# Cosine attention and a feed-forward layer on one core: each batch's values, second products and first products regrouped into one visit

## The chip, the cores and the metric

The kernel runs on one core of a Trainium2 chip. A core has TensorE (matrix products, called PE in the profile, with its weight loads as PEld), VectorE (DVE), ScalarE (ACT), GpSimd (POOL) and SyncE (SP, which here only starts transfers). The metric is the device time of one execution in microseconds (us), as the median of several runs; lower is better. Before the change it is 428.98 us, the median of 3 runs (428.75, 428.98 and 428.99).

## The reference

Per batch (8) and head (12), with 448 tokens of 64 numbers each, rows of q and k are divided by their norms, scores are their products divided by tau = 0.1, and a softmax over the keys weighs the rows of v. The heads side by side give 3584 rows of 768 numbers, which go through two matrix products with a leaky relu between them.

```python
q_n = q / (np.linalg.norm(q, axis=-1, keepdims=True) + 1e-06)
k_n = k / (np.linalg.norm(k, axis=-1, keepdims=True) + 1e-06)
scores = np.matmul(q_n, k_n.transpose(0, 1, 3, 2)) / tau
scores = scores - np.max(scores, axis=-1, keepdims=True)
attn = np.exp(scores)
attn = attn / (np.sum(attn, axis=-1, keepdims=True) + 1e-09)
attn_out = np.matmul(attn, v)
...
h = x @ w_in                       # 768 to 2048
g = np.maximum(0.01 * h, h)
return (g @ w_out).astype(np.float32)   # 2048 to 768
```

## The kernel before, in words

**Units of work.** Two heads make a pair, or slot; there are 6 slots a batch, 48 in all, numbered through. Two slots make a quad: 3 a batch, 24 in all. A batch's 448 keys are three tiles of 128 and a rest of 64. `s0` stands below for a batch's first slot, `b * NPAIR`.

**Norms of a slot.** `load_qk` (L122) loads q and k. POOL squares them (`squares`, L158, recorded at L167), after a small copy (`hold`, L484) that waits until the slot before is normed. DVE sums the squares (`sums`, L171, recorded at L178). ACT takes the roots with a Ln and an Exp (`roots`, L182: L185, L186). DVE divides (`normalise`, L192: L197, L198, L202). From slot 12 on, a transfer on SP's queue transposes the result into a tile qkT (`transposes`, L228: L234), of which there are five. `norm(s)` (L645) is all of this for slot s, the loads three slots on and the squares of the next slot. In it, sums come directly before the roots.

**Key tiles.** `key_tiles` (L247) multiplies keys with queries into two PSUM banks per tile (recorded at L259) and then has ACT take the exponential of each (L271) into pe, or pr for the rest. A tile of 128 keys uses the array as 64 rows by 128 columns, two heads side by side. The tile called (p, 3) holds the 64 rest keys of slots p-1 and p, as four products of 64 rows by 64 columns.

**Values.** `attend(j)` (L570) does quad j: `totals` sums the exponentials over keys (4 x 4 strips of 128 rows by 32 columns, recorded at L282), ACT inverts them with a Ln and an Exp (L293, L294), `products` multiplies with the values in two groups of 4 x 4 strips (L282 too), and `scale` (L308: L313) has DVE multiply both into xT.

**The two products of the feed-forward layer.** Chunk c holds 384 (c even) or 512 (c odd) of the tokens; chunk 2m+1 also takes the rest rows of batch 2m. `first(c, m)` (L327) is one of 16 blocks of hidden units: 6 products of 128 rows by 128 columns (L336), whose leaky relu ACT takes (L343). `second(c, ts, half)` (L362) does half of the outputs of a block of 128 tokens: 16 products of 128 by 128 (L366), copied out by DVE (L377). `both_halves` (L392) does the same block in another form: each product is split into two of 64 rows, side by side (L415), 32 in the first part and 32 in the second; in the second part the row halves change banks, so its first product waits for the last of the first part. DVE then copies both halves out (L425), and SP stores them (L388).

**PSUM.** `banks` (L79) deals out the eight banks, always the ones that were dealt or given back longest ago; two next to each other for a key tile, for `attend` and for `both_halves`. A token block of `both_halves` keeps its two until they are copied out.

**The order.** Every engine runs its instructions in the order in which the code issues them, which is written out by hand. Batches 0 to 2 have stages of their own (L514 to L694). From batch 3 on, a loop (L704) makes three visits per batch. The first belongs to the last quad of the batch before. Each visit is: `attend` of a quad; two key tiles; the first part of a token block; three key tiles; its second part; two key tiles, the last of them with rest keys; then a `norm`, half of the visit's first products of the chunk of the batch before (5 or 6 blocks), another `norm`, and the other half. Where a chunk has four token blocks, the fourth goes between the first products as two `second`. Behind the last batch come the last quad, the remaining token blocks as `second`, and the last chunk.

SP's queue holds, in that order, transposes, loads and stores. A transfer waits there for its data and for its buffer, and those behind it wait with it. POOL's queue holds squares and the loads of values (`load_v`, L141; `load_v_rem`, L148).

Of the kernel before, what the change touches and what calls it, by code (L numbers as in the profile page):

```python
# [8 lines left out]
F32 = mybir.dt.float32  # L9
# [7 lines left out]
def kernel(  # L17
# [10 lines left out]
    nc = tc.nc  # L28
    B, H, S, D = q.shape
    N_tok, D_model = out.shape  # L30
# [6 lines left out]
    NPAIR = H // 2  # L37
    NSLOT = B * NPAIR
    NQ = NPAIR // 2
    KT = D_model // 128  # L40
    MT = D_ff // 128
    HALF = D_model // 2
# [6 lines left out]
    MT_APART = 1  # L49
# [7 lines left out]
    smp = ctx.enter_context(tc.tile_pool(name="small", bufs=3))  # L57
    qnp = ctx.enter_context(tc.tile_pool(name="qn", bufs=3))
    qtp = ctx.enter_context(tc.tile_pool(name="qt", bufs=5))
    pep = ctx.enter_context(tc.tile_pool(name="pe", bufs=3))  # L60
    prp = ctx.enter_context(tc.tile_pool(name="pr", bufs=2))
    rbp = ctx.enter_context(tc.tile_pool(name="rb", bufs=2))
    xtp = ctx.enter_context(tc.tile_pool(name="xt", bufs=2))
    htp = ctx.enter_context(tc.tile_pool(name="ht", bufs=2))
    osp = ctx.enter_context(tc.tile_pool(name="os", bufs=3))
# [13 lines left out]
    def banks(count, keep=None, which=None):  # L79
        lo, hi = (0, 8) if not deals["apart"] else (0, 4) if count == 2 else (4, 8)  # L80
        x = which if which is not None else min(
            (i for i in range(lo, hi, count) if not set(range(i, i + count)) & set(sum(kept.values(), []))),
            key=lambda i: max(age[i : i + count]),
        )
        deals["n"] += 1
        age[x : x + count] = [deals["n"]] * count
        if keep:
            kept[keep] = list(range(x, x + count))
        return ps[:, x] if count == 1 else ps[:, x : x + count]

    def given_back(keep):
        deals["n"] += 1
        for i in kept.pop(keep):
            age[i] = deals["n"]
# [44 lines left out]
    vb, vrb = {}, []  # L139

    def load_v(j):  # L141
        if j >= B * NQ:
            return
        b, jj = divmod(j, NQ)
        vb[j] = vbp.tile([128, 4, 3, D], BF16, name="v_b")
        gp.dma_start(out=vb[j], in_=main(v, b, 4 * jj, 4))

    def load_v_rem(b):  # L148
        if b >= B:
            return  # L150
        r = v[b, :, MAIN:S].rearrange("(j g) p d -> g p j d", g=4)
        for g in range(4):
            lo = 64 * (g // 2)
            gp.dma_start(out=vrb[b % 2][lo : lo + 64, :, g], in_=r[g])
# [16 lines left out]
    def sums(s, parts=(0, 1)):  # L171
        if s >= NSLOT:
            return
        if s not in ss:
            ss[s] = smp.tile([128, 14], F32, name="ss")
        for i in parts:
            o = ss[s][:, 0:8] if i == 0 else ss[s][:, 8:14]
            nc.vector.tensor_reduce(  # L178
                o.rearrange("p (h t) -> p h t", h=2), sqs[s][i], axis=AX.X, op=ALU.add
            )  # L180
# [61 lines left out]
    pe, pr = {}, {}  # L242
# [79 lines left out]
    def chunk_cols(c):  # L322
        return (0, MAIN) if c % 2 == 0 else (MAIN, 512)
# [25 lines left out]
    osb = {}  # L349
# [12 lines left out]
    def second(c, ts, half):  # L362
        c0, n = chunk_cols(c)
        po2 = banks(1)
        for m in range(MT):
            nc.tensor.matmul(  # L366
                out=po2[:, :HALF],
                lhsT=hT[c][:, m, ts * 128 : (ts + 1) * 128],
                rhs=w_out_sb[:, m, half * HALF : (half + 1) * HALF],
                start=(m == 0), stop=(m == MT - 1),  # L370
            )
        if half == 0:
            osb[c, ts] = osp.tile([128, D_model], F32, name="osb")
        o = osb[c, ts]
        last = c == B - 1 and ts == n // 128 - 1
        cut = HALF // 2 if last and half == 1 else HALF
        nc.vector.tensor_copy(out=o[:, half * HALF : half * HALF + cut], in_=po2[:, :cut])  # L377
        if cut < HALF:
            nc.scalar.copy(out=o[:, half * HALF + cut : (half + 1) * HALF], in_=po2[:, cut:HALF])
        if half == 1 or last:  # L380
            store(o, c, c0 + ts * 128, half * HALF if last else 0, (half + 1) * HALF, cut < HALF)

    def store(o, c, x, lo, hi, apart=False):
        end, row = x + 128, 0
        while x < end:
            dst, cnt = rows_of(c, x, end)
            eng = nc.scalar if apart and row else nc.sync
            eng.dma_start(out=dst[:, lo:hi], in_=o[row : row + cnt, lo:hi])  # L388
            x += cnt
            row += cnt  # L390

    def both_halves(c, ts):  # L392

        state = {}

        def part(n):
            if n == 0:
                state["po"] = banks(2, ("rows", c, ts))  # L400
            po2 = state["po"]
            last = {}
            for m in range(MT):
                for h in range(2):
                    rows, half = slice(64 * h, 64 * h + 64), h ^ n
                    if n == 1 and m == 0:
                        tc.add_manual_dep(
                            nc.tensor.nop().ins,
                            state["last"][half].ins.name,
                            mybir.DependencyInfo(  # L410
                                mybir.DependencyClass.Sync, mybir.DependencyReason.DATA
                            ),
                            reason="the other rows' products in this bank",
                        )
                    last[half] = nc.tensor.matmul(  # L415
                        out=po2[:, half, :HALF],
                        lhsT=hT[c][rows, m, ts * 128 : (ts + 1) * 128],
                        rhs=w_out_sb[rows, m, half * HALF : (half + 1) * HALF],
                        start=(n == 0 and m == 0), stop=(n == 1 and m == MT - 1),
                    )  # L420
            state["last"] = last
            if n == 1:
                o = osp.tile([128, D_model], F32, name="osb")
                for half in range(2):
                    nc.vector.tensor_copy(  # L425
                        out=o[:, half * HALF : (half + 1) * HALF], in_=po2[:, half, :HALF]
                    )
                given_back(("rows", c, ts))
                store(o, c, chunk_cols(c)[0] + ts * 128, 0, D_model)

        return lambda: part(0), lambda: part(1)


    work = {}
    for c in range(B):
        c0, n = chunk_cols(c)
# [77 lines left out]
    for s in range(NPAIR):  # L514
        j = s // 2 - 1 if s >= 2 else None
# [54 lines left out]
    def attend(j):  # L570
        totals(j)
        po = banks(2)
        for e in range(2):
            products(j, e, po[:, e])
        for e in range(2):
            scale(j, e)
# [68 lines left out]
    def norm(s):  # L645
        if s >= NSLOT:
            return
        sums(s)
        roots(s)
        normalise(s)  # L650
        transposes(s)
        load_next(s)
        hold(qn[s][:, 6, 0, 0:1])
        squares(s + 1)

    queue = []
    for b in range(1, 3):
# [37 lines left out]

    visits = [
        (-1, [(0, 0), (0, 1)], [(0, 2), (1, 0), (1, 1)], [(1, 2), (1, 3)]),
        (0, [(2, 0), (2, 1)], [(2, 2), (3, 0), (3, 1)], [(3, 2), (3, 3)]),  # L700
        (1, [(4, 0), (4, 1)], [(4, 2), (5, 0), (5, 1)], [(5, 2), (5, 3)]),
    ]
    tiles_left = [(1, ts) for ts in range(MT_APART, 4)]
    for b in range(3, B):  # L704
        firsts = [fn for _, fn in work[b - 1][:MT]]
        more = []
        if len(tiles_left) > len(visits):
            c, ts = tiles_left.pop()
            more = [lambda half=half: second(c, ts, half) for half in range(2)]
        for i, (at, *parts) in enumerate(visits):  # L710
            j, rows = b * NQ + at, both_halves(*tiles_left.pop(0))
            attend(j)
            load_v(j + 2)
            if at == 1:
                load_v_rem(b + 1)
            for n, part in enumerate(parts):
                key_tiles([(b * NPAIR + p, ki) for p, ki in part])
                if n < 2:
                    rows[n]()
            fill_in = [firsts.pop(0) for _ in range(len(firsts) // (len(visits) - i))]  # L720
            if more:
                fill_in.insert(2, more.pop(0))
            norm(b * NPAIR + 2 * i + 4)
            for n, fn in enumerate(fill_in):
                if n == len(fill_in) // 2:
                    norm(b * NPAIR + 2 * i + 5)
                fn()
        tiles_left = [(b - 1, ts) for ts in range(chunk_cols(b - 1)[1] // 128)]
    attend(B * NQ - 1)
    for c, ts in tiles_left:  # L730
        for half in range(2):
            second(c, ts, half)
    for _, fn in work[B - 1]:
# [36 lines left out]
```

## Time and profile before

| what | us |
|---|---|
| median of 3 runs | 428.98 |
| the profiled execution | 428.73 |
| its span, first to last instruction | 426.8 |
| TensorE busy | 413.7 (97%) |
| ACT busy | 255.5 (60%) |
| DVE busy | 197.0 (46%) |
| POOL busy | 137.0 (32%) |

The profile is that of one execution. A row of groups gives an engine's line in the code, the operation, what it writes and reads, how many, the busy time in all and the mean of one in ns, and after a bar the time in which the engine sat idle before them. A row of the timeline gives start, duration, engine and line; neighbours of the same kind are merged. Matmuls overlap, so that a duration is longer than the distance to the next start, and a busy TensorE may still be held up. The granted clock of TensorE is 0.998 of full speed in the mean. These are the largest groups of TensorE and ACT on the page:

```profile
L336 PE MATMUL ps<-xT,w_in_sb 128*128 128x384 bf16 (+1 forms) x768 | 151.6, 353 | 0.5 <-DVE xT L313 0.5
L271 ACT ACTIVATE pe<-ps 128x896 bf16<-128x896 f32 x144 | 123.5, 915 | 40.7 <-PE ps L259 38.9
...
L415 PE MATMUL ps<-w_out_sb,hT 64*128 64x384 bf16 x960 | 83.9, 323 | 0.3
```

### The profile page before, as it was taken

The page shows a single profiled execution, that of the slowest core. Times are in us where ns is not written, and L with a number is a line of the kernel's source. Part 1 is how long each engine was busy: PE and PEld are TensorE (multiplying, and loading weights), DVE is VectorE, ACT ScalarE, POOL GpSimd, SP SyncE. Part 2 cuts the span into 40 slices and gives each one's busy share as a digit, 9 for nine tenths or more (in the row PEclk, how much of TensorE's full clock was granted, in tenths as well). Part 3 has the DMA queues.
Part 4 walks back from the last instruction along what each step waited for, and adds up shares of the span by engine and source line. Part 5 has one row for each costly group of instructions (what it writes and reads, how often), then busy time and mean ns, then how long its engine had stood idle before and what let it go on. Part 6 is the DMA issues. An engine that isn't in the chain of part 4 may idle for free.

```text
span 426.8 us, 9601 instructions
## 1 busy us (share of the span) xinstructions
PE 413.7 (97%) x3809; PEld 214.0 (50%) x3809; DVE 197.0 (46%) x412; ACT 255.5 (60%) x448; POOL 137.0 (32%) x208
## 2 busy tenths in 40 slices
PE   7689999999999999999999999999999999999995
PEld 2234455544455555554555555554545555554563
DVE  5885867646554455436436354445445310210021
ACT  3987785678855856765765746856855746114300
POOL 4767533543461253242441252241441000000000
PEclk9999999999999999999999999999999999999999
DMA  7999997998586668574764677755753421010022
GB/s 173 187 245 228 211 217 134 185 197 160 130 137 144 135 122 157 128 139 113 131 144 104 106 171 116 153 124 119 139 99 65 41 75 38 37 76 1 2 74 74
DMA packets 102892, 53.71 MB, mean 126 GB/s; under 512 B 68928, under 2 KB 97856, under 8 KB 102848
## 3 DMA queue, kind: packets, MB, share of 16 engines
q1 hardware_dynamic: 77296, 40.98, 41.8%
q0 software_dynamic: 25056, 11.80, 21.5%
q8 instruction: 29, 0.48, 0.5%
q10 hardware_dynamic: 496, 0.33, 0.2%
q14 instruction: 15, 0.12, 0.1%
HBM read 45.61 MB, written 11.01 MB: 133 GB/s over the span
## 4 chain that ended last, share of the span: by engine, by line
PE 87%; DVE 5%; ACT 2%; DMA 2%; POOL 1%; SPq 1%; issue 1%; POOLq 0%; DVEq 0%
PE ps L336 32%; PE ps L415 18%; PE ps L366 16%; PE ps L282 12%; PE ps L259 8%; DVE qn L202 2%; POOL sq L167 1%; DVE ss L178 1%; DMA q_h<-in_q_dram 1%; PE ps L216 1%; DMA q_h<-in_k_dram 1%; ACT hT L343 1%; SPq L131 1%; DVE osb L425 0%; ACT pe L271 0%
## 5 line engine op out<-in xcount | busy, mean ns | idle before, releaser
L336 PE MATMUL ps<-xT,w_in_sb 128*128 128x384 bf16 (+1 forms) x768 | 151.6, 353 | 0.5 <-DVE xT L313 0.5
L271 ACT ACTIVATE pe<-ps 128x896 bf16<-128x896 f32 x144 | 123.5, 915 | 40.7 <-PE ps L259 38.9
L336 PEld LDWEIGHTS <-w_in_sb 128*128 128x128 bf16 x768 | 73.0, 98 | 71.5 <-issue 6.7
L343 ACT ACTIVATE hT<-ps 128x384 bf16<-128x384 f32 (+1 forms) x128 | 64.3, 538 | 41.8 <-PE ps L336 41.2
L415 PE MATMUL ps<-w_out_sb,hT 64*128 64x384 bf16 x960 | 83.9, 323 | 0.3
L366 PE MATMUL ps<-w_out_sb,hT 128*128 128x384 bf16 x416 | 70.0, 326 | 0.0
L486 POOL CAST seen<-qn 128x1 f32<-128x1 bf16 x47 | 8.6, 184 | 186.6 <-DVE qn L202 186.5
L178 DVE TENSOR_REDUCE ss<-sq 128x8 f32<-128x512 f32 (+1 forms) x96 | 57.3, 615 | 23.6 <-POOL sq L167 20.6
L415 PEld LDWEIGHTS <-hT 64*128 64x128 bf16 x960 | 49.0, 94 | 32.7 <-issue 2.4
L366 PEld LDWEIGHTS <-hT 128*128 128x128 bf16 x416 | 40.1, 98 | 28.2 <-issue 2.1
L259 PE MATMUL ps<-qkT 64*128 64x448 bf16 (+1 forms) x384 | 49.2, 357 | 3.7 <-ACT pe L271 2.3
L167 POOL TENSOR_TENSOR sq<-q_h 128x512 f32<-128x512 f32 x46 | 47.7, 1038 | 3.6 <-DMA q_h<-in_k_dram 2.8
L425 DVE COPY osb<-ps 128x384 f32<-128x384 f32 x30 | 15.3, 553 | 72.2 <-PE ps L415 72.2
L185 ACT ACTIVATE ss<-ss,tiny 128x14 f32<-128x14 f32 x48 | 14.9, 311 | 49.1 <-DVE ss L178 49.0
L377 DVE COPY osb<-ps 128x384 f32<-128x384 f32 (+1 forms) x26 | 14.3, 549 | 58.2 <-PE ps L366 58.2
L313 DVE TENSOR_TENSOR xT<-ps,rb 128x448 bf16<-128x448 f32 x48 | 27.8, 619 | 28.3 <-ACT rb L294 28.3
L167 POOL TENSOR_TENSOR sq<-k_h 128x384 f32<-128x384 f32 x46 | 37.8, 822 | 0.0
L282 PE MATMUL ps<-pe,v_b 128*32 128x448 bf16 x576 | 35.6, 353 | 0.0
L202 DVE TENSOR_TENSOR qn<-q_h,r 128x512 bf16<-128x512 f32 x48 | 33.5, 698 | 1.6
L259 PEld LDWEIGHTS <-qkT 64*128 64x128 bf16 (+1 forms) x384 | 15.4, 96 | 33.5 <-issue 24.9
L202 DVE TENSOR_TENSOR qn<-k_h,r 128x384 bf16<-128x384 f32 x48 | 26.5, 552 | 0.0
L197 DVE TENSOR_SCALAR ss<-ss 128x14 f32<-128x14 f32 x46 | 9.4, 204 | 32.8 <-ACT ss L186 32.6
(43 smaller groups left out, 233.8 us busy)
## 6 DMA issues: line engine op xcount, KB each, us to landing
q_h<-in_q_dram SPq DMA_DIRECT2D x48, 192.0 KB, 3.1
k_h<-in_k_dram SPq DMA_DIRECT2D x47, 192.0 KB, 3.3
out_dram<-osb SPq DMA_DIRECT2D x30, 192.0 KB, 2.7
v_b<-in_v_dram POOLq DMA_DIRECT2D x24, 192.0 KB, 5.0
out_dram<-osb SPq DMA_DIRECT2D x12, 384.0 KB, 2.5
w_in_sb<-in_moe_w_in_dram POOLq DMA_DIRECT2D x4, 768.0 KB, 9.8
w_out_sb<-in_moe_w_out_dram POOLq DMA_DIRECT2D x2, 1536.0 KB, 17.7
q_h<-in_q_dram SPq DMA_DIRECT2D x48, 32.0 KB, 3.8
```

The source lines that it names most:

```text
L167: eng.tensor_tensor(sq, x, x, op=ALU.mult)
L178: nc.vector.tensor_reduce(o.rearrange("p (h t) -> p h t", h=2), sqs[s][i], axis=AX.X, op=ALU.add)
L202: nc.vector.tensor_tensor(qn[s][:, lo:hi], x.rearrange("p h t d -> p t h d"), r[:, r0 : r0 + 2 * nt].rearrange("p (h t) -> p t h", h=2) .u ...
L259: nc.tensor.matmul(out=out[:, a, :S], lhsT=x[rows, c0:c1], rhs=x[rows, 0:S], start=True, stop=True,)
L271: nc.scalar.activation(out=dst, in_=sc[:, :, :S], func=AF.Exp, scale=inv_tau)
L282: nc.tensor.matmul(out=x[32 * g : 32 * g + 32, :S], lhsT=weights(g, ki) if ki < 3 else rem(g), rhs=pe[s][:, ki, a, :] if ki < 3 else pr[j] ...
L313: nc.vector.tensor_tensor(xT[m][:, 2 * jj + e, half * S : (half + 1) * S], pos.pop((j, e))[:, :S], rbs[j], op=ALU.mult,)
L336: nc.tensor.matmul(out=pm[:, :n], lhsT=w_in_sb[:, kt, m * 128 : (m + 1) * 128], rhs=xT[c // 2][:, kt, c0 : c0 + n], start=(kt == 0), stop= ...
L343: nc.scalar.activation(out=hT[c][:, m, :n], in_=pms.pop((c, m))[:, :n], func=AF.Prelu, alpha=0.01)
L366: nc.tensor.matmul(out=po2[:, :HALF], lhsT=hT[c][:, m, ts * 128 : (ts + 1) * 128], rhs=w_out_sb[:, m, half * HALF : (half + 1) * HALF], st ...
L415: last[half] = nc.tensor.matmul(out=po2[:, half, :HALF], lhsT=hT[c][rows, m, ts * 128 : (ts + 1) * 128], rhs=w_out_sb[rows, m, half * HALF ...
L425: nc.vector.tensor_copy(out=o[:, half * HALF : (half + 1) * HALF], in_=po2[:, half, :HALF])
```

## The change

From batch 3 on, a batch becomes one visit in three stages.

1. Values: `attend` of the three quads of the batch before (at batch 3 only of its last, since the others are done), and the loads of values. Then two tiles of rest keys, (1, 3) and (3, 3).
2. All second products of the chunk before last, by `both_halves`, which now yields after each step of two products. The 18 tiles of 128 keys are dealt out among them, most of them one at a time: with three token blocks, after steps 5, 11, 16 (two), 21 and 27 of each; with four, fewer per block. For the first three blocks, `sums` of a slot stands at the block's start and `norm` of the same slot at step 16. The fourth block takes this form too. At the end comes the third tile of rest keys, (5, 3).
3. All 16 first products of the chunk of the batch before, with three more slots' sums (at blocks 0, 5, 10) and norms (at 2, 7, 12).

`norm` no longer holds the sums. The buffers of pe go from 3 to 6 and those of pr from 2 to 3. Behind the last batch, three quads are attended instead of one. All counts of products, exponentials, copies and transfers stay.

```diff
-    pep = ctx.enter_context(tc.tile_pool(name="pe", bufs=3))
-    prp = ctx.enter_context(tc.tile_pool(name="pr", bufs=2))
+    pep = ctx.enter_context(tc.tile_pool(name="pe", bufs=6))
+    prp = ctx.enter_context(tc.tile_pool(name="pr", bufs=3))
...
+        po2 = banks(2, ("rows", c, ts))
+        last = {}
+        for n in range(2):
+            before, last = last, {}
             for m in range(MT):
                 for h in range(2):
...
+                yield
+        o = osp.tile([128, D_model], F32, name="osb")
...
     def norm(s):
         if s >= NSLOT:
             return
-        sums(s)
         roots(s)
...
+    tokens = [(1, ts) for ts in range(MT_APART, 4)]
     for b in range(3, B):
...
+        for j in range(b * NQ - 1 if b == 3 else (b - 1) * NQ, b * NQ):
             attend(j)
+        for j in range(b * NQ, (b + 1) * NQ):
+            if j not in vb:
+                load_v(j)
+        load_v_rem(b + 1)
+        s0 = b * NPAIR
+        tiles = [(s0 + p, ki) for p in range(NPAIR) for ki in range(3)]
+        key_tiles([(s0 + 1, 3), (s0 + 3, 3)])
+        for i, (c, ts) in enumerate(tokens):
+            if i < 3:
+                sums(s0 + 4 + i)
+            if len(tokens) == 3:
+                after = {5: 1, 11: 1, 16: 2, 21: 1, 27: 1}
+            else:
+                after = {8: 1, 16: 2, 21: 1, 27: 1} if i < 2 else {8: 1, 16: 2, 24: 1}
+            for n, _ in enumerate(both_halves(c, ts), 1):
+                for _ in range(after.get(n, 0)):
+                    key_tiles([tiles.pop(0)])
+                if n == 16 and i < 3:
+                    norm(s0 + 4 + i)
+        assert not tiles
+        key_tiles([(s0 + 5, 3)])
+        for m in range(MT):
+            if m in (0, 5, 10):
+                sums(s0 + 7 + m // 5)
+            if m in (2, 7, 12):
+                norm(s0 + 7 + m // 5)
+            first(b - 1, m)
+        tokens = [(b - 1, ts) for ts in range(chunk_cols(b - 1)[1] // 128)]
+    for j in range((B - 1) * NQ, B * NQ):
+        attend(j)
+    for c, ts in tokens:
```

The lines taken out of the loop are those of the three visits, which the kernel above shows (L698 to L729).

## The prediction

> **What bounds the kernel now.** I read the page's busy times first, then its chain that ended last, then TensorE's timeline over one visit, then busy time by stretch, and last the rows of one key pair's way from ACT to its slot.
>
> ```profile
> PE 413.7 (97%) x3809; PEld 214.0 (50%) x3809; DVE 197.0 (46%) x412; ACT 255.5 (60%) x448; POOL 137.0 (32%) x208
> ...
> PE 87%; DVE 5%; ACT 2%; DMA 2%; POOL 1%; SPq 1%; issue 1%; POOLq 0%; DVEq 0%
> ```
>
> TensorE is the bound, so only what lengthens or shortens its stream counts. Its instructions stay the same; their order changes. The question is what lies between them. TensorE's timeline over a visit of batch 5 (start, duration, line, rows*columns of the array):
>
> ```profile
> 216.89 0.75 PE L282 MATMUL ps<-pe,ones 128*32 128x448 bf16 x12
> ...
> 218.98 0.36 PE L282 MATMUL ps<-pr,v_rem 128*32 128x448 bf16 x4
> 219.27 0.55 PE L259 MATMUL ps<-qkT 64*128 64x448 bf16 x4
> 219.66 2.76 PE L415 MATMUL ps<-w_out_sb,hT 64*128 64x384 bf16 x32
> 222.26 0.73 PE L259 MATMUL ps<-qkT 64*128 64x448 bf16 x6
> 222.83 2.76 PE L415 MATMUL ps<-w_out_sb,hT 64*128 64x384 bf16 x32
> 225.43 0.67 PE L259 MATMUL ps<-qkT 64*128 64x448 bf16 x6
> 226.03 2.12 PE L336 MATMUL ps<-xT,w_in_sb 128*128 128x384 bf16 x12
> ```
>
> Start to start: a key tile takes 0.19 (222.26 to 222.83, three of them), 32 matmuls of L415, side by side in pairs, 2.60 (219.66 to 222.26: 16 steps of 0.1625), four strips of L282 0.19, a 384-column matmul of L336 0.1625. Between L259 and L415, both 64*128, nothing is lost. Where the shape changes, something is: 218.98 to 219.27 is 0.29 instead of 0.19; 225.43 to 226.03 is 0.60 for two tiles (0.38), and two changes lie in it (64*128 to 64*64 for the rest tile, 64*64 to 128*128). Busy time by stretch, one stretch per visit (length, TensorE busy, clock, DMA share, GB/s):
>
> ```profile
> 122.61:136.72 14.11, 14.11 (x159) 1.00 0.71 133
> 136.72:152.00 15.28, 15.10 (x160) 1.00 0.62 130
> 152.00:168.24 16.24, 16.06 (x166) 1.00 0.81 138
> 168.24:184.15 15.91, 15.89 (x159) 1.00 0.59 131
> 184.15:199.87 15.72, 15.72 (x159) 1.00 0.64 127
> ```
>
> The first two hold the same work, and the second is 1.17 longer: stalls that "busy" hides, since long matmuls overlap them.
>
> **The change, part by part** (us; against the profiled execution, 428.73, which is span 426.8 plus 1.93 around it; the median shown is 0.25 higher).
>
> 1. *Shape changes.* A visit's steps (12 strip groups and 7 tiles at 0.189, 32 at 0.1625, here 46 more at 0.1625) are 16.27; it takes 16.72: 0.45 for its four changes, of which 0.106 is 128*32 to 64*128, 0.22 the two above, 0.10 each the return to strips (with 0.01 on the step after). 15 visits: 6.78. After, a batch has five: the return 0.10; 128*32 to 64*64 and 64*64 to 64*128, not in the trace, bounded by the nearest rows at 0.09 and 0.14 each, taken as 0.12 and 0.14, since leaving 64*64 is the dear one in the rows; the last two 0.23. With 0.59 a batch, 2.94 in all: **-3.84**. Two rest tiles in a row are not in the trace either; they are put at 0.19 like strips, at most 0.10 more. Bounds -4.2 to -3.2.
>    The Trainium skill (TensorEngine Tiling (Array Packing), Key Properties) says that a change of tiling mode drains the engine; from TensorE: Matmul & The Clock Gate, Single matmul latency, an isolated matmul pays 398 cycles, 0.166 us, beyond its columns. An estimate by that figure is 35 changes fewer x 0.166 = 5.8 saved; the rows say 0.09 to 0.14 a change, and they decide.
>
> 2. *Stalls that go.* 1.17 (136.72); 1.15 (152.00: 16.24 against 14.11 and one first product of 0.975); 0.19 each in the first visits of batches 4 (15.91 against 15.72) and 6: **-2.70**. Their cause: ACT's Ln for the norms waits 3.71 us for DVE's sums (L178), queued behind the copy L425; the Ln of the totals (L293) stands behind it until 140.05, and key tiles at 139.11 need its banks. After, sums are asked for ahead of the norm. A norm's round (Ln to next Ln) takes 5.02 (148.73 to 153.75); norms come 6.3 apart among second products and 4.88 apart among 384-column first products, so ACT falls 0.15 behind per norm there, while eight banks rotate. If that cover were gone, up to 2.7 comes back.
>
> 3. *A new wait at the first key tiles of batch 3.* Tile (3,3) needs the transposed slot 21. Before, its first reader is the second visit (136.72 on); after, it is the second tile behind attend(8), at 124.99 + 0.19 = 125.18. Its transpose on SP's queue and the landing time of L234:
>
> ```profile
> 124.38 1.24 SPq L234 DMA_TRANSPOSE qkT<-qn  x1
> ...
> DMA to landing us min/median/max: 2.9/3.0/5.5
> ```
>
>    This one took 3.36: landed 127.74, plus 0.05 release and 0.10 for weights that can't be loaded ahead. **+2.70**; behind the waiting weight load stands all of TensorE's queue. Nothing ahead of it changes. In later batches slot s0+3 is issued over 4 us earlier than needed.
>
> 4. *A new wait in batches with three tokens* (3, 4, 6). Slot s0+5 is normed half-way through token 2 and first read by dealt tile 16, half-way through token 3. From tile 9's start to tile 16's, TensorE has 0.38 + 2.60 + 0.38 + 2.60 + 0.38 + 0.19 = 6.52. The slot's way starts at the same tile: two exponentials stand ahead of its Ln.
>
> ```profile
> 109.45 0.94 ACT L271 ACTIVATE pr<-ps 128x896 bf16<-128x896 f32 x1
> 110.25 0.33 ACT L185 ACTIVATE ss<-ss,tiny 128x14 f32<-128x14 f32 x1
> ...
> 110.86 0.17 DVE L197 TENSOR_SCALAR ss<-ss 128x14 f32<-128x14 f32 x1 [1.76 <-ACT ss L186]
> ...
> 112.56 1.24 SPq L234 DMA_TRANSPOSE qkT<-qn  x1
> ```
>
>    Tile to exponential 0.42 (222.26 to 222.68), to the next 0.81, to the Ln 0.80, to DVE 0.61, to the transpose 1.70, landing 2.95, release and weights 0.15: 7.44. Late by 0.92, three times: **+2.76**. Batches with four tokens have a token more. SP's queue has a slot's loads (2.3) and a store (1.2) ahead of that transpose, both done by then. A transpose that lands in 4.1 to 5.5, as 7 of 36 do, adds 1.2 or more each.
>
> 5. *The clock.* Wait 3 leaves TensorE without a matmul from 125.33 to 127.78: 2.45. The trace has one such stretch, at its end: the last matmul ends at 422.28, and 2.44 later the granted clock halves. Stretches (length, TensorE busy, clock):
>
> ```profile
> 11.71:15.12 3.41, 1.99 (x15) 1.00 0.93 167
> 421.31:424.72 3.41, 0.97 (x6) 1.00 0.37 85
> 424.72:426.80 2.08, 0.00 (x0) 0.50 0.15 50
> ```
>
>    Idle stretches of 1.1 early on left it whole. Mine has 0.98 busy in 3.41, as the one that lost it. At the start, 512-column matmuls come 0.427 apart from 1.52 to 4.88 and 0.216 after: half the clock lasts 3.36 us once work comes, which costs 1.68. Bounds 0 and 1.68; I take **+1.68**, the row it equals, with 0.6.
>
> 6. *At nothing.* Values of three quads in a row: the third needs banks that the first's scale frees 3.33 after its start, and asks 5.3 after. The first dealt tile needs the third's scale, 0.27 before its turn. ACT has 6 exponentials and a root pair per token, 5.5 of 6.33; the tightest bank is free 0.6 early. Second half-products wait for the first's last matmul, whose semaphore event stands 0.34 after its start; two tiles give 0.54 (if not: up to 0.1 x 17). Second products of 4-token batches change shape at the same 0.1625 a step. Loads of values on POOL (3 x 0.82, 4 x 0.63) end before its next hold. More pe buffers lift two waits of 0.56 on ACT in batch 0, where TensorE waits for DVE anyway: 0 to -0.5.
>
> Sum: -3.84 - 2.70 + 2.70 + 2.76 + 1.68 = +0.60: 429.3 in the profile's terms, **429.6** against the median.
>
> **Rivals.**
> - *The clock stays.* One example of a fall, after work had ended for good, is little, and my stretch only equals it. Then -1.08: 427.9, faster. The Trainium skill (TensorE: Matmul & The Clock Gate, Part 1) gives an activity window of 3.4 us that runs free of the kernel, and lets the clock fall after an idle one. Read strictly, 2.45 is too short; the trace's last window, 0.97 busy, speaks against the strict reading.
> - *Slow transposes* (the other side). Place: slot s0+5 in batches 3, 4, 6. Price: 1.2 to 1.6 for each that lands in over 4. It decides from one, if the clock falls (430.8 to 431.2), and from two if not (430.3). For: 7 of 36, P(at least one of three) about 0.45 with several loads in flight; against: at this point the loads are down, which I let halve it.
> - *ACT or banks become the bound among dealt tiles*: slack 0.6, so a root pair 1 us late stalls each token, up to 17 x 0.5: 430 to 434.
> - *Fewer waits than counted* (the round is quicker, slot 21 lands in 2.9): 426.8 to 427.5. That the shape changes don't fall as counted is excluded: the order is fixed.
>
> **How the numbers follow.** Forecast (clock falls, transposes normal) 0.36, own range 428.8 to 430.4; clock stays 0.27; slow transposes 0.23; ACT or banks 0.08; fewer waits 0.06. 0.2% is 0.86 us, about what can be told. Faster: 0.75 of the second and the last, 0.25. Within: 0.7 of the forecast, the rest of the second, 0.04 others: 0.36. Slower: the rest, 0.39. Range 427.4 to 431.8.
>
> **What would show it.** TensorE: 0.1 gaps at five places a batch; one gap of about 2.6 ahead of tile (3,3) of batch 3, released by SP's transpose; 0.9 ahead of tile 16 in batches 3, 4, 6, none in 5 and 7; matmuls at twice their step for 3.4 us behind the first gap. Wrong if gaps stand before L415 or at other tiles, or if 136 to 168 keeps its stalls.

## The result, and the profile after

The changed kernel takes 427.85 us (median of 20 runs, 426.68 to 429.31) where the kernel before takes 428.98 (20 runs beside them, 428.62 to 429.50). The ratio is 0.9976, with a 95% interval of 0.9966 to 0.9986. So it is faster by 1.1 us, a quarter of a percent; the forecast of 429.6, no change that can be told, was wrong, though its range holds the time. Also new is the spread: 2.6 us instead of 0.9.

The profiled execution took 429.06 (span 427.2), near the long end of the 20. Its page, busy times and the chain that ended last:

```profile
PE 410.6 (96%) x3873; PEld 213.9 (50%) x3873; DVE 197.5 (46%) x412; ACT 262.6 (61%) x448; POOL 136.8 (32%) x208
...
PE 87%; DMA 6%; DVE 3%; SPq 1%; issue 1%; ACT 1%; POOL 0%; POOLq 0%; DVEq 0%
```

TensorE has the same 87% of the chain; DMA has gone from 2% to 6%. Nearly 3% of the chain are four transposes, 12 us in all, each of which ends in a wait of TensorE in batches 3, 4 and 6; the other transfers on the chain are loads in the stages before the loop. The row of TensorE's groups for key tiles, before and after, shows those waits: more than half of its idle time (behind the bar) is now a wait for transposed slots.

```profile
L259 PE MATMUL ps<-qkT 64*128 64x448 bf16 (+1 forms) x384 | 49.2, 357 | 3.7 <-ACT pe L271 2.3 <-DVE qkT L240 1.3
...
L259 PE MATMUL ps<-qkT 64*128 64x448 bf16 (+1 forms) x384 | 53.4, 358 | 7.6 <-DMA qkT<-qn 4.0 <-ACT pe L271 2.3 <-DVE qkT L240 1.0
```

TensorE's timeline shows the two places: the front of batch 3, then the sixteenth dealt tile of that batch; the last two rows are the front of batch 4, where nothing waits (L412 is the L415 of before):

```profile
125.40 0.57 PE L259 MATMUL ps<-qkT 64*64 64x448 bf16 x6
128.10 0.38 PE L259 MATMUL ps<-qkT 64*64 64x448 bf16 x2 [2.13 <-DMA qkT<-qn]
...
129.76 2.13 PE L412 MATMUL ps<-w_out_sb,hT 64*128 64x384 bf16 x12
131.68 0.58 PE L259 MATMUL ps<-qkT 64*128 64x448 bf16 x2
...
145.74 0.35 PE L259 MATMUL ps<-qkT 64*128 64x448 bf16 x2
146.76 0.36 PE L259 MATMUL ps<-qkT 64*128 64x448 bf16 x2 [0.66 <-DMA qkT<-qn]
...
172.97 0.57 PE L259 MATMUL ps<-qkT 64*64 64x448 bf16 x8
173.48 0.99 PE L412 MATMUL ps<-w_out_sb,hT 64*128 64x384 bf16 x10
```

Tile (3,3) waits for slot 21, as forecast; half of it belongs to slot 20 and runs before the wait, so six products, not four, stand ahead. From the first rest tile to L412 it is 3.01 (125.40 to 128.41), and 0.51 in batch 4 (172.97 to 173.48): the wait costs 2.50. Behind it, 12 products of L412 and the start of the next tile lie 1.92 apart (129.76 to 131.68); a full clock needs 6 x 0.1625 = 0.98. Tile 16 waits in batches 3, 4 and 6, by starts 0.83, 0.76 and 0.77 beyond the step, and not in 5 and 7. Stretches around the first wait (length, TensorE busy, the other engines, clock):

```profile
125.64:129.06 3.42, 1.29 (x16) 0.51 (x12) 1.95 (x4) 1.46 (x2) 3.42 (x5) 1.00 0.88 164
129.06:132.47 3.41, 3.41 (x26) 1.65 (x22) 0.00 (x0) 1.46 (x3) 2.09 (x4) 0.50 1.33 182
```

The clock is at half from 129.06 to 132.47 and nowhere else between its first full grant at 6.18 and 426. These times lie on a grid: 36 stretches of 3.413 fit between 6.18 and 129.06, and the half clock lasts one more. In all 14 traces of this case the clock changes only at such steps from the first full grant, which comes between 4.2 and 7.3 us. Below, a stretch of the grid means one of these 3.41 us.

Batch by batch, from the first `attend` of one to that of the next, the changed kernel's stretches, under them the sum of those of before:

```profile
123.01:166.05 43.04, 40.24 (x385) 22.42 (x385) 23.00 (x49) 29.47 (x50) 16.93 (x27) 0.96 0.74 149
166.05:214.49 48.44, 47.85 (x481) 24.27 (x480) 23.01 (x48) 33.45 (x55) 18.31 (x28) 1.00 0.65 130
214.49:262.25 47.76, 47.76 (x545) 27.45 (x544) 23.82 (x50) 31.91 (x55) 15.02 (x24) 1.00 0.64 132
262.25:310.71 48.46, 47.85 (x481) 24.23 (x481) 23.01 (x48) 33.45 (x55) 18.48 (x28) 1.00 0.62 129
310.71:358.46 47.75, 47.75 (x545) 27.45 (x544) 12.83 (x26) 30.32 (x47) 4.23 (x7) 1.00 0.31 57
...
sum 240.00, PE 239.59 PEld 128.54 DVE 107.84 ACT 153.82 POOL 73.22; mean PE 47.92 PEld 25.71 DVE 21.57 ACT 30.76 POOL 14.64
```

The changed kernel's sum to 235.45. Two `attend` of 12 strip groups each (2 x 12 x 0.189 = 4.54) have moved behind the loop, so this stands against 239.99 of equal work; before, it was 240.00 (122.61 to 362.61). (One count didn't stay: TensorE has 3873 instructions where it had 3809, since the fourth token block of two batches is now split into halves, 64 products for 32 each time. Each pair of halves takes the same 0.1625.) In this one execution all that the regrouping gained went back into waits and clock. Most others must have lost less, and the experiments ask which of the losses is not always there.

### The profile page after: what moved, and what is told of

Read it like the earlier page. It is cut to its first block, busy times and chain, and to the rows that moved or that the text cites. A ratio compares the mean times of both kernels' runs of the same rounds, so it can differ in the third digit from the quotient of the medians.

```text
span 427.2 us, 9731 instructions
## 1 busy us (share of the span) xinstructions
PE 410.6 (96%) x3873; PEld 213.9 (50%) x3873; DVE 197.5 (46%) x412; ACT 262.6 (61%) x448; POOL 136.8 (32%) x208
## 4 chain that ended last, share of the span: by engine, by line
PE 87%; DMA 6%; DVE 3%; SPq 1%; issue 1%; ACT 1%; POOL 0%; POOLq 0%; DVEq 0%
PE ps L336 34%; PE ps L412 20%; PE ps L366 14%; PE ps L282 12%; PE ps L259 7%; DMA qkT<-qn 3%; DMA q_h<-in_q_dram 3%; DVE qn L202 2%; DMA q_h<-in_k_dram 1%; SPq L131 1%; PE ps L216 1%; ACT pe L271 0%; DVE ss L197 0%; DVE qkT L240 0%; DVE xT L313 0%
## 5 line engine op out<-in xcount | busy, mean ns | idle before, releaser
L336 PE MATMUL ps<-xT,w_in_sb 128*128 128x384 bf16 (+1 forms) x768 | 149.2, 353 | 0.9 <-DVE xT L313 0.9
L343 ACT ACTIVATE hT<-ps 128x384 bf16<-128x384 f32 (+1 forms) x128 | 68.4, 542 | 71.2 <-PE ps L336 70.6
L412 PE MATMUL ps<-w_out_sb,hT 64*128 64x384 bf16 x1088 | 102.6, 326 | 0.0
L412 PEld LDWEIGHTS <-hT 64*128 64x128 bf16 x1088 | 53.0, 95 | 39.5 <-issue 3.2
L178 DVE TENSOR_REDUCE ss<-sq 128x8 f32<-128x512 f32 (+1 forms) x96 | 58.2, 616 | 27.2 <-POOL sq L167 23.6
L259 PE MATMUL ps<-qkT 64*128 64x448 bf16 (+1 forms) x384 | 53.4, 358 | 7.6 <-DMA qkT<-qn 4.0
L366 PE MATMUL ps<-w_out_sb,hT 128*128 128x384 bf16 x352 | 58.9, 326 | 0.0
L366 PEld LDWEIGHTS <-hT 128*128 128x128 bf16 x352 | 33.8, 98 | 24.0 <-issue 2.1
L377 DVE COPY osb<-ps 128x384 f32<-128x384 f32 (+1 forms) x22 | 12.0, 547 | 51.7 <-PE ps L366 51.7
L271 ACT ACTIVATE pr<-ps 128x896 bf16<-128x896 f32 x24 | 21.6, 917 | 8.2 <-PE ps L259 8.2
L293 ACT ACTIVATE rb<-ps 128x448 f32<-128x448 f32 x24 | 13.1, 544 | 19.4 <-PE ps L282 19.4
```

What stands on the lines that cost most here:

```text
L178: nc.vector.tensor_reduce(o.rearrange("p (h t) -> p h t", h=2), sqs[s][i], axis=AX.X, op=ALU.add)
L259: nc.tensor.matmul(out=out[:, a, :S], lhsT=x[rows, c0:c1], rhs=x[rows, 0:S], start=True, stop=True,)
L271: nc.scalar.activation(out=dst, in_=sc[:, :, :S], func=AF.Exp, scale=inv_tau)
L293: nc.scalar.activation(rb, sm[:, :S], func=AF.Ln)
L336: nc.tensor.matmul(out=pm[:, :n], lhsT=w_in_sb[:, kt, m * 128 : (m + 1) * 128], rhs=xT[c // 2][:, kt, c0 : c0 + n], start=(kt == 0), stop= ...
L343: nc.scalar.activation(out=hT[c][:, m, :n], in_=pms.pop((c, m))[:, :n], func=AF.Prelu, alpha=0.01)
```

## The experiments

**Theory** after the result: the terms of the prediction hold, but the clock falls behind wait 3 only in some executions. **Rivals**: the fall is always there and the landings of transposes vary; or a term is mis-sized by 1 to 2 us, above all the shape changes or the stalls that go. All medians below stand beside 9 to 17 runs of the kernel before, with medians of 428.92 to 429.11.

**1. `e1_rest_late`: wait 3 taken away.** From the changed kernel:

```diff
-        key_tiles([(s0 + 1, 3), (s0 + 3, 3)])
+        key_tiles([(s0 + 1, 3)] if b == 3 else [(s0 + 1, 3), (s0 + 3, 3)])
...
-        key_tiles([(s0 + 5, 3)])
+        key_tiles([(s0 + 3, 3), (s0 + 5, 3)] if b == 3 else [(s0 + 5, 3)])
```

> Edit: in batch 3 alone, rest tile (3,3) goes from the front to the end of the second products, beside (5,3). Theory (wait plus clock): in the profile of the changed kernel tile (3,3) stood 2.30 us beyond its step and the clock then ran at half for 3.41 us, which costs up to 1.7. With the tile away from there neither happens: the clock stays whole in every run, and the time is 2.30 below the runs of the changed kernel that kept the clock (427.2): 424.9, with a spread of under 1 us as the kernel before has it (428.62 to 429.50) instead of 2.6. Rival (the wait is only passed on): the next tile that needs a late slot or a bank takes it over, and the median stays at 426.5 or more. Second rival (the spread has nothing to do with this place): the median falls by 2.3 from 427.85 to 425.5 and the spread stays at 2.6.

Measured: 424.82 (424.54 to 425.06), ratio 0.9906 (0.9893 to 0.992). The time and the narrow spread are the theory's; both rivals fall. The expectation took the wait for 2.30, where the rows above give 2.50; from 427.2 to 424.82 it is 2.4. One detail was wrong: the mean clock is 0.994 to 1.0, not always whole. The trace shows a half clock at 13.73, in the stage of batch 0, where TensorE waits for other engines anyway. (The profiled execution of experiment 6 has such a fall at 14.46 and is the shortest of its eleven.) A mean clock alone therefore doesn't say whether a fall cost anything; the place does.

**2. `e2_busy_wait`: the wait kept, the idleness taken away.**

```diff
-        key_tiles([(s0 + 1, 3), (s0 + 3, 3)])
+        key_tiles([(s0 + 1, 3)])
+        if b == 3:
+            wm = banks(2)
+            for i in range(12):
+                nc.tensor.matmul(
+                    out=wm[0:64, i % 2, :S], lhsT=warm[0:64, :64], rhs=warm[0:64, :S],
+                    start=True, stop=True,
+                )
+        key_tiles([(s0 + 3, 3)])
```

> Edit: the wait stays, but 12 idle products of 64x64 and 448 columns (12 x 0.189 = 2.27 us) stand in front of tile (3,3) of batch 3, so that TensorE works while it waits; they write two banks that nobody reads. Theory (the clock falls because TensorE has no work): the clock stays whole in every run and the time is that of the changed kernel's runs with a whole clock, 427.0 to 427.4, without its slow end. Rival (the fall is a matter of chance or the lower median has another cause): the clock still falls in some runs, and the median stays near 427.85 with a spread of 2.6. If the half clock costs nothing, the median stays and only the clock changes.

Measured: 426.80 (426.69 to 427.26), ratio 0.9954 (0.9941 to 0.9968). The long end of the changed kernel (up to 429.31) is gone and the wait is still paid. Five runs alone could miss the longer kind by chance: at its share of 10 in 26 (below) the odds are about 0.09, and under 0.01 with the five of experiment 7. So what made the long end was TensorE's idleness, that is the clock; landings alone, which this edit leaves as they were, don't make it.

**3. `e3_norm_first`: the waits at tile 16 taken away.**

```diff
+                if n == 16 and i < 3:
+                    norm(s0 + 4 + i)
                 for _ in range(after.get(n, 0)):
                     key_tiles([tiles.pop(0)])
-                if n == 16 and i < 3:
-                    norm(s0 + 4 + i)
```

> Edit: at step 16 of a token block the norm is issued ahead of the two key tiles, so that two exponentials less stand before its Ln on ACT. Theory (the round of slot s0+5 is late at dealt tile 16 by 0.77 to 0.83 in batches 3, 4 and 6, 2.35 in all, for that reason): the two exponentials are 1.6, so the wait goes in all three, unless a transpose lands late; 427.85 - 2.35 = 425.5, the wait at (3,3) and the half clock stay. Rival (ACT or the banks have no slack): the exponentials that now come later hold up banks, and TensorE waits for them instead: 427 or more.

Measured: 424.39 (424.22 to 424.91), ratio 0.9898 (0.9885 to 0.9912). All three waits are gone, and only the one at (3,3) is left (1.80 idle by the trace). The time is 1.1 under the expectation, since none of these four runs shows the longer kind of time. From the first `attend` of batch 3 to the first behind the loop, this trace takes 231.05 (122.62 to 353.67) and the changed kernel's shorter kind (experiment 5) 233.41 (122.84 to 356.25): 2.36, as expected. In this profiled execution the grid cut the idle time in two:

```profile
122.70:126.12 3.42, 2.87 (x54) 1.24 (x54) 3.27 (x8) 1.81 (x3) 1.52 (x4) 1.00 0.68 77
126.12:129.53 3.41, 2.16 (x26) 1.23 (x28) 1.14 (x2) 1.76 (x3) 3.41 (x6) 1.00 0.81 165
129.53:132.94 3.41, 3.41 (x44) 2.00 (x42) 1.42 (x4) 3.16 (x7) 1.24 (x3) 1.00 1.32 200
```

Neither part was enough, and the clock stayed whole. Experiment 5 shows that 1.77 in one stretch is not enough either.

**4. `e4_both`**: edits 1 and 3 together.

> Edit: both of the edits before, rest tile (3,3) of batch 3 late and the norm ahead of the tiles. Theory: the gains add up, 427.2 - 2.30 - 2.35 = 422.6 with a whole clock and a spread under 1 us; what is left of the change is then the shape changes (-3.84 by the prediction) and the stalls that go (-2.70): 428.98 - 6.54 = 422.4. Rival (one wait hides behind the other, or a third comes up): 424 or more. If shape changes had cost much less than counted, the sum of the two estimates would not meet: 422.6 from above would be 424 to 426.

Measured: 422.45 (422.26 to 422.75), ratio 0.9852 (0.9838 to 0.9865). The gains add up, and this kernel beats both. In its trace TensorE waits for nothing from batch 3 to batch 7; the five stretches sum to 228.95, or 233.49 with the two `attend`: 6.51 less than before, against 3.84 + 2.70 = 6.54 in terms 1 and 2.

**5. `e5_after_again`**: the changed kernel once more, no edit.

> Edit: none, the changed kernel once more. The traces so far show the half clock coming in pieces of 3.41 us on a grid that begins at another time in each execution; it followed stretches with TensorE busy for 0.97, 1.28, 1.66 and 1.85 us of 3.41, and not those with 1.64 (once), 1.90, 1.97, 1.99 and 2.17. Theory (the grid decides): the wait ahead of tile (3,3), about 2 us idle, costs the clock only when some 1.6 or more of it fall into one stretch of the grid, which is so in about (3.41 - 2.1 + 2 x 0.5) / 3.41 = 0.68 of the executions. The times are then of two kinds, about 427.0 to 427.5 without the fall and 428.5 to 429.3 with it, and the profiled execution shows which it is. Rival (the clock falls at this wait always, and what varies is the landing of transposes): every trace has the half clock behind tile (3,3), and fast executions have shorter waits.

Measured: 426.97 (426.46 to 428.79), ratio 0.9956 (0.9942 to 0.9971): five runs at 426.46 to 427.25 and one at 428.79. This profiled execution (426.88) is of the shorter kind. The front of its batch 3, and the stretches around the same wait:

```profile
125.23 0.57 PE L259 MATMUL ps<-qkT 64*64 64x448 bf16 x6
127.56 0.38 PE L259 MATMUL ps<-qkT 64*64 64x448 bf16 x2 [1.77 <-DMA qkT<-qn]
127.87 0.99 PE L412 MATMUL ps<-w_out_sb,hT 64*128 64x384 bf16 x10
...
124.14:127.55 3.41, 1.65 (x34) 0.57 (x22) 3.23 (x6) 1.73 (x3) 2.56 (x4) 1.00 0.55 91
127.55:130.97 3.42, 3.41 (x40) 1.97 (x42) 0.04 (x1) 2.55 (x3) 3.42 (x6) 1.00 0.92 165
```

With 1.77 idle in one stretch and 1.65 busy, the clock stayed. So the wait at this place, in the same code, costs the clock in one execution and not in another, and the rival of a sure fall is out. The threshold in the expectation was too low: 1.6 idle is not enough.

What saved the clock here the trace alone doesn't tell. The wait is shorter than in the first trace of the changed kernel (1.77 idle instead of 2.13), because the transpose landed after 2.91 us instead of 3.27. And the grid would have cut a longer one, since a stretch ends at 127.55, just where this wait does. Over the 14 traces this transpose lands after 2.9 to 3.4 us, in three of them after more than 3.2. So two things vary from one execution to the next, the landing and the grid. No trace has an idle time of 2 us or more that the grid cuts in two, and which share each has in the two kinds of times stays open.

**6. `e6_sums_early`: one part of the change alone, in the kernel before.**

```diff
     def norm(s):
...
-        sums(s)
...
             attend(j)
+            sums(b * NPAIR + 2 * i + 4)
             load_v(j + 2)
...
             norm(b * NPAIR + 2 * i + 4)
+            sums(b * NPAIR + 2 * i + 5)
```

> Edit: the kernel before with one part of the change alone: norm no longer holds the sums; those of a visit's first norm stand behind its values, those of the second behind the first norm. Theory (sums queued behind the copy on DVE cause the four stalls of 1.17, 1.15, 0.19 and 0.19): 428.9 - 2.70 = 426.2. What is then left to the version with both waits removed (422.45) is the shape changes: 426.2 - 422.45 = 3.75, against -3.84 in the prediction. Rival (the stalls come from banks or from ACT's pace, and the sums only show beside them): 428.5 or more.

Measured: 428.13 (427.66 to 428.38), ratio 0.9977 (0.9968 to 0.9986). A miss: only 0.93 of 2.70. Its second and third visit of batch 3 and the first of batch 4 last:

```profile
136.68:151.64 14.96, 14.81 (x160) 8.48 (x159) 7.63 (x16) 9.72 (x18) 4.77 (x9) 1.00 0.62 133
151.64:167.57 15.93, 15.78 (x167) 9.07 (x166) 8.44 (x18) 10.20 (x19) 8.07 (x13) 1.00 0.84 144
167.57:183.28 15.71, 15.66 (x158) 7.83 (x158) 8.05 (x17) 10.19 (x19) 4.77 (x7) 1.00 0.59 132
```

The 0.19 in batch 4 is gone (15.91 to 15.71) and 0.3 each of the two large stalls, but 0.84 and 0.83 stay (14.96 over 14.12; 15.93 over 14.12 and a block of 0.975). DVE's timeline at the first says what the sums wait for there; the second row is the same place in the kernel before:

```profile
136.75 1.34 DVE L178 TENSOR_REDUCE ss<-sq 128x8 f32<-128x512 f32 x2 [1.41 <-POOL sq L167]
...
137.10 1.34 DVE L178 TENSOR_REDUCE ss<-sq 128x8 f32<-128x512 f32 x2 [1.41 <-POOL sq L167]
```

Not for a copy on DVE, but for POOL's squares, in the kernel before as well. The prediction had read only ACT's row, whose last releaser is L178, and not gone one step further back.

**7. `e7_half_busy`**: as 2, with `range(6)`.

> Edit: the changed kernel with 6 idle products instead of 12 in front of tile (3,3) of batch 3: TensorE works for 1.1 us of the wait and is idle for about 1.1. Theory (a fall needs some 1.6 us idle in one stretch of 3.41): the clock never falls there, and the time is that of 12 products, 426.7 to 427.3. Rival (any longer idle time may cost the clock, or the dummies help by something else than being work): times up to 429 appear, and the median is 427.5 or more.

Measured: 426.74 (426.64 to 427.27), ratio 0.9949 (0.9937 to 0.9961), as with 12. Half the cover is enough: in the trace the stretch with the wait has 2.77 busy of 3.41, and the clock stays. So it is not idleness as such that counts, but how much of it there is in one stretch.

**8. `e8_rest_end`: two shape changes fewer per batch.** From `e4_both`, with seven buffers of qkT:

```diff
-        key_tiles([(s0 + 1, 3)] if b == 3 else [(s0 + 1, 3), (s0 + 3, 3)])
...
-        key_tiles([(s0 + 3, 3), (s0 + 5, 3)] if b == 3 else [(s0 + 5, 3)])
+        key_tiles([(s0 + 1, 3), (s0 + 3, 3), (s0 + 5, 3)])
```

> Edit: the version with both waits removed, and now in every batch all three rest tiles stand together at the end of the second products; the transposed slots get seven buffers instead of five, since slots s0 and s0+1 are read later. Theory (a shape change costs 0.09 to 0.13): per batch 128*32 to 64*64 (0.103) and 64*64 to 64*128 (0.10) go and 128*32 to 64*128 (0.106) comes, 0.10 less, five times: 422.45 - 0.5 = 421.95. Rival (three rest tiles in a row hold six banks, and ACT must take three exponentials, 2.4 us, before the first products get going): TensorE waits some 0.5 a batch: 422.5 to 425.

Measured: 422.54 (422.10 to 422.72), ratio 0.9847 (0.9834 to 0.9859): no gain over 422.45. The changes did go, and 0.06 per batch is gained where there are four token blocks (47.70 against 47.76). Where there are three, a rest tile starts 0.18 beyond its step and the batch is longer (47.76 against 47.68). In batch 3 a transposed slot came late at a dealt tile, which the edit did not mean to touch (0.49 by starts). The rival, a hold-up by banks among the three tiles, fits the place, but no run took it away; it stays argued.

**9. `e9_norms_apart`: the rest of the stalls.** From `e6_sums_early`:

```diff
                 if n < 2:
                     rows[n]()
+                if n == 0:
+                    norm(b * NPAIR + 2 * i + 4)
...
-            norm(b * NPAIR + 2 * i + 4)
             sums(b * NPAIR + 2 * i + 5)
```

> Edit: the kernel before with the sums early, and a visit's first norm moved up behind the first part of its token block, so that the two norms of a visit in batch 3 stand 2.6 + 0.57 + 0.38 + 1.95 = 5.5 us apart on TensorE instead of 1.95. In the run with the sums early alone (428.13) two visits of batch 3 kept 0.85 and 0.84 over their work: there the sums of the second norm's successor wait 1.41 for POOL's squares, since two norms follow each other faster than a round of 5.02 through ACT, DVE and POOL. Theory (that spacing makes the rest of the stalls): they go, 428.13 - 1.69 = 426.4. Then only shape changes lie between this kernel and the version of the changed kernel without waits: 426.4 - 422.45 = 3.95, against -3.84 in the prediction. Rival (the norm now stands ahead of key tiles' exponentials and holds up banks, or the stalls come from banks in any case): 428 or more.

Measured: 426.24 (425.87 to 426.64), ratio 0.9935 (0.9922 to 0.9947). The visits that `e6_sums_early` left long:

```profile
136.56:150.68 14.12, 14.12 (x161) 7.78 (x160) 7.43 (x16) 10.27 (x18) 4.77 (x8) 1.00 0.72 160
150.68:165.77 15.09, 15.09 (x165) 8.37 (x165) 7.44 (x16) 10.76 (x19) 7.26 (x12) 1.00 0.74 139
```

14.12 is the undisturbed visit, 15.09 that and one block: the stalls are gone. Over the whole loop it is 237.30 (122.44 to 359.74), 2.70 less than before. The stalls came from two norms standing closer on TensorE (1.95) than a norm's round (5.02), and only 1.0 of the 2.70 from where the sums were asked for. Between this kernel and `e4_both`, neither with a wait in the loop, lie 426.24 - 422.45 = 3.79 by the medians and 237.30 - 233.49 = 3.81 by the loops in the traces: the shape changes, against 3.84.

**10 and 11. `e10_small_same` and `e11_small_shape`: the price of a change by itself.** From `e4_both`; R is 128 in the one and 64 in the other:

```diff
+        wm = banks(1, ("small", b))
...
             first(b - 1, m)
+            if m < MT - 1:
+                nc.tensor.matmul(
+                    out=wm[0:R, :128], lhsT=warm[0:R, :R], rhs=warm[0:R, :128],
+                    start=True, stop=True,
+                )
```

> Edit: the version with both waits removed (422.45), with one small idle product of 128*128 and 128 columns behind each of the first 15 of a batch's 16 blocks of first products, 75 in all; they write a bank that nobody reads. It is the control for the next one. Both theories: a product of 128 columns takes 128/384 of 0.1625, 0.054, so 75 x 0.054 = 4.1: 426.5; up to 0.1 more each if a short product can't hide its weight load: 434.

> Edit: the same 75 small products, but of 64*64, so that each brings two changes of shape. Theory (the rows' prices: 0.126 into 128*128, about 0.09 to 0.10 into 64*64): 75 x 0.22 = 16.5 above the control, 443 if the control is 426.5. Rival (an isolated product pays 0.166, as the Trainium skill, TensorE: Matmul & The Clock Gate, Single matmul latency, would have it for each change): 75 x 0.33 = 24.9 above the control. Second rival (changes are nearly free, and the gain of the change came from elsewhere): within 4 of the control.

Measured: 426.51 (426.13 to 426.96), ratio 0.994 (0.9926 to 0.9953), and 443.36 (443.08 to 443.52), ratio 1.0332 (1.0318 to 1.0346). 16.85 us for 150 changes are 0.112 each. TensorE's timeline of `e11_small_shape`:

```profile
160.22 0.24 PE L723 MATMUL ps<-warm 64*64 64x128 bf16 x1
160.39 1.15 PE L336 MATMUL ps<-xT,w_in_sb 128*128 128x384 bf16 x6
161.47 0.24 PE L723 MATMUL ps<-warm 64*64 64x128 bf16 x1
```

From one small product to the next lie 1.25: six steps of 0.1625 (0.975), the product (0.054), and 0.22 for two changes. The Trainium skill (TensorE: Matmul & The Clock Gate, Single matmul latency) led to an estimate of 0.166 per change, if each were paid as an isolated product is; the runs here say 0.112.

**12. `e12_long_wait`: the fall made certain.** From the changed kernel, the two first rest tiles of batch 3 ahead of `attend(8)`:

```diff
     for b in range(3, B):
+        s0 = b * NPAIR
+        if b == 3:
+            key_tiles([(s0 + 1, 3), (s0 + 3, 3)])
         for j in range(b * NQ - 1 if b == 3 else (b - 1) * NQ, b * NQ):
...
-        key_tiles([(s0 + 1, 3), (s0 + 3, 3)])
+        if b > 3:
+            key_tiles([(s0 + 1, 3), (s0 + 3, 3)])
```

> Edit: the changed kernel with the two first rest tiles of batch 3 moved ahead of attend(8) instead of behind it. Tile (3,3) then waits from about 123.3 to 127.8, some 4.5 us idle instead of 2.1, with attend(8) queued behind it. Theory (the grid decides, and a stretch of 3.41 needs about 2 us idle): wherever the grid lies, one stretch holds at least 2.2 of 4.5, so the clock falls in every execution; the time is that of the changed kernel without a fall (427.0) plus 2.3 of more wait plus 1.7: 431.0, all within 1 us of each other, and no mean clock above 0.996. Rival (the fall is a matter of chance whatever the length of the wait): two kinds of times again, 429.3 and 431. Second rival (a half clock costs less than 1.7): 429.3 to 430.5 with the half clock in the trace.

Measured: 431.45 (430.69 to 432.01), ratio 1.0053 (1.004 to 1.0067). All five are near 431 and have mean clocks of 0.991 to 0.996; there is no shorter kind left. The spread is 1.3, a little over what was expected, and the stretches show one reason:

```profile
122.94:126.35 3.41, 0.58 (x7) 0.14 (x6) 2.12 (x5) 0.92 (x1) 1.50 (x4) 1.00 0.62 68
126.35:129.77 3.42, 2.11 (x22) 0.89 (x26) 0.00 (x0) 0.92 (x1) 2.28 (x3) 0.50 0.86 178
129.77:133.18 3.41, 3.41 (x40) 1.26 (x34) 0.83 (x2) 1.12 (x2) 0.05 (x1) 0.50 1.22 209
```

The wait reached into the half-clock stretch, which was then busy for only 2.11, and the clock stayed at half for a second one. Where the grid lies otherwise, one stretch may be lost; that would explain the two runs near 430.8, but no trace shows it.

## Why the prediction was wrong, point by point

The shape changes, the waits and the fall of the clock were all there, at the places named. What failed is **step 5, the clock, taken as +1.68**: it was read as one cost that comes or doesn't with the kernel, and "my stretch", 0.98 busy of 3.41, as one that begins where the wait does. The two traces of the changed kernel have 1.29 busy, and the clock fell, and 1.65 busy, and it stayed. The half clock is granted in pieces of 3.41 us on a grid that starts elsewhere in each execution, and how long TensorE is busy in one piece decides (the cases stand in the last section); this wait lies so near the border that some executions pay and others don't. That the grid can save the clock by cutting a wait of about 2.1 in two would follow, but no trace has that case: in `e5_after_again` the wait was shorter as well. When the fall comes the price is right: 3.41 us of matmuls at twice their step, 1.7, and the medians of the two kinds of times lie 1.5 apart. It didn't come in most executions: 11 of the first 20 runs lie at 426.68 to 427.93 and 9 at 428.33 to 429.31; with the six of `e5_after_again` it is 16 to 10. (That each of the 10 fell at this place is shown by one trace, and by experiments 1, 2, 7 and 12 for the group.) The median of the 20 is the border of the shorter kind. The Trainium skill (TensorE: Matmul & The Clock Gate, Part 1) has the free-running window, and the traces agree (3.413); the prediction weighed it only for whether 2.45 is long enough, not for what it can mean, namely that one kernel has two times.

A smaller share is in two terms that were sized too high:

| term | predicted | measured |
|---|---|---|
| 1 shape changes | -3.84 | -3.81 by the loops, -3.79 by the medians (`e9_norms_apart` to `e4_both`) |
| 2 stalls that go | -2.70 | -2.70 by the loops, -2.87 by the medians (to `e9_norms_apart`); cause named in part |
| 3 wait at (3,3) | +2.70 | +2.5 in the profiled execution, +2.1 in `e5_after_again` |
| 4 waits at tile 16 | +2.76 | +2.36 (0.83, 0.76, 0.77) |
| 5 half clock | +1.68 | +1.7 or 0 |

- *Step 1* is right to 0.05, and so is the price of the changes that the trace had not shown (0.12 and 0.14 taken; 0.10 each measured, 0.02 on a neighbour of the same shape).
- *Step 2* is right in size and wrong in part in its cause. The sums queued behind the copy were worth 1.0; the rest was the distance of two norms. The change removed both, so the sum held by luck of the edit.
- *Step 3*: the transpose landed after 3.27 and 2.91 us instead of 3.36, and in both traces the products start 0.04 behind the landing, where release and weights were put at 0.15. That half of tile (3,3) runs before the wait saves nothing: the other half still takes 0.31 to L412 (128.10 to 128.41), as a whole rest tile does in `e4_both` (0.32, 125.43 to 125.75).
- *Step 4*: at the places named and in the batches named; 0.09 to 0.16 less each.
- *Step 6* holds in `e4_both`: with both waits gone, TensorE waits for nothing in these batches, so neither banks nor ACT are the bound.

Terms 1 to 4 by the measured column give -3.81 - 2.70 + 2.1 + 2.36 = -2.05 for an execution in which the clock stays (426.9), and with the longer wait and the clock -1.65 + 1.7 = +0.05 (429.0) for one in which it falls. The loops of the two traces say -2.05 (233.41 + 4.54 against 240.00) and -0.01, and the medians of the two kinds are 427.2 and 428.8. The rival "the clock stays" named 427.9, which is the median by number but not by reason: its kind of execution takes 427.2.

## What to carry to other kernels

Where an idle time of TensorE comes near 2 us, don't ask whether the clock will fall but in what share of the executions, and forecast two times; a profile of one execution shows one of them. Cover such a wait with other work (here half of it was enough), or move the tile that waits: this regrouping was worth 6.5 us, and two small moves kept it (422.45). When a stall's releaser has itself waited, follow the chain one more step back before naming the cause.

## What the runs showed of the hardware

- After its first full grant the clock fell behind every stretch with up to 1.40 us of 3.41 busy (among them 0.58, 0.80, 0.97, 1.29 and 1.40), and stayed after 1.64 (the end of `e3_norm_first`) and 1.65 (the wait of `e5_after_again`). In batch 0, with many small gaps between matmuls whose ends are modelled, it fell at up to 1.85 and stayed from 1.90. So not a whole stretch of idleness is needed: outside batch 0, somewhere between 1.8 and 2.0 us of it in one stretch.
- After a fall, a stretch that was busy for 2.11 at half clock did not bring it back (`e12_long_wait`); one that was busy for 2.82 did (`e1_rest_late`, 13.73 to 17.14), and so did one that was busy throughout.
- The same transpose, at the same place, landed after 2.9 to 3.4 us over the 14 traces.
- A change of the array's shape costs 0.09 to 0.13 by the rows, 0.112 in the mean of 150.
